# Two x loads trade queues at the start of a fused attention and MLP kernel, and ScalarE's first DMA waits for a GpSimd memset

## The chip, the cores and the metric

The kernel runs on one core of a Trainium2 chip. The metric is the device time of one execution, in microseconds (us).

## What is computed

The inputs are x (2048 tokens of 640 values, bf16), wqkv (640 x 1920), wo (640 x 640), w1 (640 x 1728) and w2 (1728 x 640). The reference, cut to what matters:

```python
xn = layernorm(x)                       # over the 640 values, eps 1e-5, no gain or bias
q, k, v = split_heads(xn @ wqkv)        # 32 heads of 20
phi = lambda t: where(t > 0, t + 1, exp(t)) + 1e-6
kv  = einsum("bhsd,bhse->bhde", phi(k), v)
z   = einsum("bhsd->bhd", phi(k))
o   = (phi(q) @ kv) / (phi(q) . z + 1e-6)
s   = merge_heads(o) @ wo
g   = silu(relu(xn @ w1) @ w2)
out = x + s * g
```

It is linear attention (no softmax over positions) times a gate that an MLP makes, plus the residual.

## The kernel before

The 2048 tokens are 16 tiles of 128 tokens, called t, in four groups j of 512. The 640 values are five blocks of 128, called c or k. Up to eight x tiles are held in `xin` (`x_load`, line 336); xn transposed, so that the values are on the partitions, is `xnT`.

Everything is written in one program order by hand. A small scheduler (`Sched`) keeps, for each engine, the list of its operations in that order, and works out from the tiles that an operation reads and writes which semaphores it has to wait for. It reorders nothing: an engine or a DMA queue executes its own list in order and stops at the first wait that is not met. `extra` adds a wait for a given operation. DMAs are issued from SyncE's queue (SP) or from ScalarE's (ACT); what stands behind a waiting issue on the same engine waits too, ScalarE's own computation included.

The start, which is what the change and the prediction speak of, goes as follows.

- GpSimd sets constants, the first of them `onesM`, 128 x 128 ones (line 344), which TensorE reads only much later, in `z_col`; then the identity that the transposes need, and two more.
- The first loads are issued: x0, x1, x2, the first part of w1 (three of the 128-column blocks f, 480 KB), the second part (two blocks, 320 KB), x3.
- `fill(9)` (line 355): nine matmuls of ones, whose result is not used, while the loads are under way.
- For tiles 0 to 3 the mean of each token is computed alone: `T_mean` (tile 0 on VectorE, line 424; tiles 1 to 3 on ScalarE, line 420). `center` subtracts it (VectorE, line 431), `T_pe` transposes the tile on TensorE (line 437), `T_copy` brings it to `xnT` (lines 444 and 447). The division by the deviation is made up for later.
- `H_first` multiplies the first tiles with the blocks of w1 that have landed (`H_mm`, line 545): tile 0 with blocks 0 to 2, tile 1 with blocks 0 to 2, then, with the second part, blocks 3 and 4.
- The load of the K columns of wqkv is issued when tile 0 has been centred (`held`), and the third part of w1 when tile 2 has been centred. The other loads stand behind these on SyncE's queue.

The order on ScalarE in this stretch is: its two DMA issues, the load of its function table, `T_mean(1)`, two `T_copy`, `T_mean(2)`, `T_mean(3)`, `T_copy`. On VectorE: `T_mean(0)`, `center(0)` in two pieces, `center(1)`, two `T_copy`, `center(2)` and so on. On TensorE: the fill, the transposes of tile 0 and tile 1, `H_first` for tiles 0 and 1.

After that come the K projection with its exponentials, the Q projection and the rest of the MLP's first half, then the sums over the tokens, the MLP's second half, and the output, tile by tile.

Of the kernel before, what the change touches and what calls it, by code (L numbers as in the profile page):

```python
# [211 lines left out]
def bass_recurrent_scan__linear_attn_block__dense_activation_relu__prompt_kernel(  # L212
# [82 lines left out]
    onesM = nc.alloc_sbuf_tensor("onesM", [P, P], bf)  # L295
# [24 lines left out]
    sc = Sched(nc, NDS)  # L320
    nds = [0]

    def dma(E, fn, R=(), W=(), extra=()):
        i = nds[0]
        nds[0] += 1
        return sc.dma(E, fn, i, R=R, W=W, extra=extra)

    def tok(t):
        return slice(P * t, P * (t + 1))
# [4 lines left out]
    def x_load(t, extra=(), E="SP"):  # L334
        sl = t % XR
        return dma(E, lambda eng: eng.dma_start(xin[:, sl, :], x2[tok(t), :]), W=[("xin", sl)], extra=extra)
# [4 lines left out]

    cones = nc.const_aps.tensor(1.0, [P, P], bf)
    cwide = nc.const_aps.tensor(1.0, [P, 512], bf)
    sc.op("POOL", lambda eng: eng.memset(onesM[:, :], 1.0), W=[("onesM",)])
    sc.op("POOL", lambda eng: eng.memset(ident[:], 0.0), W=[("ident",)])
    sc.op("POOL", lambda eng: eng.affine_select(out=ident[:], in_=ident[:], compare_op=ALU.not_equal,
                                                fill=1.0, base=0, pattern=[[-1, P]], channel_multiplier=1),
# [14 lines left out]
    def w1_load(i, extra=(), E="SP"):  # L362
        w_load(w1_sb[:, :, W1C[i]:W1C[i + 1]], B_w1[:, W1C[i]:W1C[i + 1]], ("w1", i), extra, E)

    def w1_part(f):
        return [i for i in range(NP) if W1C[i] <= P * f < W1C[i + 1]][0]

    x_load(0)
    x_load(1, E="ACT")
    x_load(2)  # L370
    w1_load(0, E="ACT")
    w1_load(1)
    x_load(3)
# [335 lines left out]
    for j in range(1, J):  # L709
# [11 lines left out]
        for n, (kind, jj, f) in enumerate(blocks):  # L721
# [19 lines left out]
            else:  # L741
                if n == 0:
                    for t in range(4):
# [4 lines left out]
                        W=[("wo", 0)], extra=[last_norm[0]])  # L748
                    dma("SP", lambda eng: eng.dma_start(wo_sb[0:VR, VC - 1, :], A_wo[D - VR:D, :]),
                        W=[("wo", 1)], extra=[last_norm[0]])  # L750
# [11 lines left out]
    for a in range(2):  # L762
# [3 lines left out]
            W=[("w2", a)], extra=[lastX])  # L766
    for u in range(2):
        dma("SP", lambda eng, u=u: eng.dma_start(w2l[64 * u:64 * (u + 1), :], B_w2[NF * P:FF, :]),
            W=[("w2l", u)], extra=[lastX])
# [235 lines left out]
```

## Time and profile before

| what | before |
|---|---|
| time, median of 3 runs | 221.51 us (221.26 to 221.65) |
| the profiled execution's own time | 221.12 us |
| its span (first to last instruction) | 219.4 us |
| TensorE busy | 215.5 us, 98% |
| VectorE, ScalarE, GpSimd busy | 114.4, 87.5 and 43.5 us |
| DMA moved | 24.51 MB, mean 112 GB/s |

The times in the profile's rows are microseconds from the start of the span. In a row of the timeline the first number is the start, the second the time from there to the end of the last of the merged instructions; `PE` is TensorE's matmuls and `PEld` its weight loads, `SPq` and `ACTq` are the DMA issues on SyncE's and ScalarE's queues. Matmuls overlap, so a busy TensorE is not one at its peak. Brackets give the idle time of the engine before the row, and what ended it.

In a row of DMA issues the last number is the median time from issue to landing. In a row of the table of stretches stand, after the stretch and its length, the busy times of TensorE's matmuls, TensorE's weight loads, VectorE, ScalarE and GpSimd with their instructions in brackets, the clock that TensorE was granted, the busy share of the DMA engines, and GB/s. In the rows of the DMA queues, q1 is SyncE's queue and q10 ScalarE's, with packets, MB and the share of the 16 DMA engines' time.

### The profile page before, as it was taken

The page shows a single profiled execution, that of the slowest core. Times are in us where ns is not written, and L with a number is a line of the kernel's source. Part 1 is how long each engine was busy: PE and PEld are TensorE (multiplying, and loading weights), DVE is VectorE, ACT ScalarE, POOL GpSimd, SP SyncE. Part 2 cuts the span into 40 slices and gives each one's busy share as a digit, 9 for nine tenths or more (in the row PEclk, how much of TensorE's full clock was granted, in tenths as well). Part 3 has the DMA queues.
Part 4 walks back from the last instruction along what each step waited for, and adds up shares of the span by engine and source line. Part 5 has one row for each costly group of instructions (what it writes and reads, how often), then busy time and mean ns, then how long its engine had stood idle before and what let it go on. Part 6 is the DMA issues. An engine that isn't in the chain of part 4 may idle for free.

```text
span 219.4 us, 3577 instructions
## 1 busy us (share of the span) xinstructions
PE 215.5 (98%) x1489; PEld 134.2 (61%) x1489; DVE 114.4 (52%) x196; ACT 87.5 (40%) x143; POOL 43.5 (20%) x66
## 2 busy tenths in 40 slices
PE   8999999999999999999999999999999999999994
PEld 2975654555545554444477778777767776777673
DVE  2778857789676999987700007503322222314053
ACT  4587765576656575555421114531021102110300
POOL 2153101279024998600000000000000000000001
PEclk9999999999999999999999999999999999999999
DMA  6996581350012206800079968377110110000002
GB/s 212 300 382 155 127 225 57 71 45 6 0 30 60 33 1 121 167 3 0 0 228 362 261 202 326 93 241 269 60 63 1 60 33 30 30 31 33 30 30 90
DMA packets 28812, 24.51 MB, mean 112 GB/s; under 512 B 11812, under 2 KB 28156, under 8 KB 28796
## 3 DMA queue, kind: packets, MB, share of 16 engines
q1 hardware_dynamic: 27852, 23.53, 37.6%
q10 hardware_dynamic: 944, 0.75, 1.1%
q8 instruction: 11, 0.18, 0.3%
q14 instruction: 5, 0.04, 0.1%
HBM read 15.75 MB, written 5.24 MB: 96 GB/s over the span
## 4 chain that ended last, share of the span: by engine, by line
PE 96%; DMA 1%; DVE 1%; issue 0%
PE psT L845 26%; PE psT L545 26%; PE psT L891 10%; PE psT L790 10%; PE psT L462 10%; PE psT L530 10%; DMA reg<-in_A_x_dram 1%; PE psT L861 1%; PE psT L567 1%; PE psT L801 1%; PE psT L812 1%; PE psT L437 1%; PE psT L648 1%; DVE ek L424 0%; DVE reg L906 0%; DVE reg L898 0%
## 5 line engine op out<-in xcount | busy, mean ns | idle before, releaser
L545 PE MATMUL psT<-reg 128*128 128x512 bf16 (+1 forms) x335 | 61.7, 331 | 0.0
L845 PE MATMUL psT<-reg,hT 128*128 128x320 bf16 x416 | 60.1, 299 | 0.0
L845 PEld LDWEIGHTS psT<-reg,hT 128*128 128x128 bf16 x416 | 40.4, 98 | 16.4 <-issue 1.1
L545 PEld LDWEIGHTS psT<-reg 128*128 128x128 bf16 x335 | 28.5, 98 | 25.6 <-issue 0.4
L913 DVE TENSOR_TENSOR reg<-psT,reg 128x640 bf16<-128x640 f32 x15 | 12.4, 825 | 54.0 <-PE psT L891 54.0
L552 ACT ACTIVATE hT<-psT 128x512 bf16<-128x512 f32 x52 | 30.7, 599 | 15.8 <-PE psT L545 15.7
L879 ACT ACTIVATE reg<-psT 128x640 bf16<-128x640 f32 (+1 forms) x13 | 8.4, 661 | 44.3 <-PE psT L845 24.9
L898 POOL TENSOR_TENSOR reg<-reg 128x256 bf16<-128x256 bf16 x1 | 0.7, 668 | 124.4 <-DVE reg L906 124.4
L530 PE MATMUL psT<-reg 128*128 128x512 bf16 x100 | 24.9, 379 | 0.0
L462 PE MATMUL psT<-reg 128*128 128x320 bf16 x160 | 24.2, 299 | 0.0
L471 POOL TENSOR_TENSOR zacc<-zacc,reg 128x640 f32<-128x640 f32 x16 | 23.7, 1484 | 1.9 <-DVE reg L505 1.0
L891 PE MATMUL psT<-reg,pqT 128*128 128x320 bf16 (+2 forms) x165 | 24.0, 295 | 0.0
L790 PE MATMUL psT<-reg 128*128 128x320 bf16 x160 | 21.9, 299 | 0.0
L462 PEld LDWEIGHTS psT<-reg 128*128 128x128 bf16 x160 | 15.5, 98 | 8.3 <-DVE ek L489 0.3
L891 PEld LDWEIGHTS psT<-reg,pqT 128*128 128x128 bf16 x165 | 16.0, 98 | 5.8
L790 PEld LDWEIGHTS psT<-reg 128*128 128x128 bf16 x160 | 15.7, 98 | 6.2
L540 DVE SCALAR_TENSOR_TENSOR pqT<-er 128x512 bf16<-128x512 bf16 x20 | 17.1, 854 | 0.7
L530 PEld LDWEIGHTS psT<-reg 128*128 128x128 bf16 x100 | 9.7, 98 | 11.6 <-DVE er L538 0.6
L537 ACT ACTIVATE er<-psT 128x512 bf16<-128x512 f32 x20 | 12.0, 598 | 8.9 <-PE psT L530 8.1
L538 DVE TENSOR_SCALAR er<-psT 128x512 bf16<-128x512 f32 x20 | 13.6, 678 | 3.1 <-ACT er L537 3.1
L395 DVE BATCH_NORM_STATS2 stats<-reg 128x6 f32<-128x320 bf16 x32 | 13.9, 477 | 1.0 <-DMA reg<-in_A_x_dram 1.0
L505 DVE TENSOR_TENSOR reg<-ek 128x640 bf16<-128x640 bf16 x16 | 13.5, 843 | 1.5 <-ACT ek L496 1.0
(63 smaller groups left out, 133.9 us busy)
## 6 DMA issues: line engine op xcount, KB each, us to landing
rscr<-rden SPq DMA_DIRECT2D x4, 640.0 KB, 10.7
reg<-rscr SPq DMA_DIRECT2D x5, 512.0 KB, 6.1
reg<-in_A_x_dram SPq DMA_DIRECT2D x4, 640.0 KB, 6.9
reg<-in_A_x_dram SPq DMA_DIRECT2D x15, 160.0 KB, 3.3
out_dram<-reg SPq DMA_DIRECT2D x15, 160.0 KB, 1.8
reg<-in_A_wqkv_dram SPq DMA_DIRECT2D x2, 800.0 KB, 6.6
reg<-in_B_w_dram SPq DMA_DIRECT2D x1, 1120.0 KB, 5.7
reg<-in_B_w_dram SPq DMA_DIRECT2D x1, 960.0 KB, 8.2
```

What stands on the lines that cost most here:

```text
L395: sc.op("DVE", lambda eng, a=a: eng.bn_stats(stats[:, t, a, :], xv[:, HN * a:HN * (a + 1)]), R=[("xin", t % XR)], W=[("stats", t, a)])
L462: fns.append(lambda eng, a=a, k=k: eng.matmul(ps[b + a][:, 0:HN], lhsT=xnT[:, k, tok(t)], rhs=wqk[:, k, D + HN * a:D + HN * (a + 1)], star ...
L471: sc.op("POOL", lambda eng: eng.tensor_tensor(out=zacc[:, :], in0=zacc[:, :], in1=pk[:, t, :], op=ALU.add), R=[("zacc",), ("pk", t)], W=[( ...
L505: sc.op("DVE", lambda eng: eng.tensor_tensor(out=pk[:, t, :], in0=e_, in1=r_, op=ALU.add), R=[("ek_e", es), ("ek_r", es)], W=[("pk", t)])
L530: sc.group("PE", [(lambda eng, k=k: eng.matmul(ps[b], lhsT=wqk[:, k, P * f:P * (f + 1)], rhs=rhs(k), start=(k == 0), stop=(k == C - 1))) f ...
L538: sc.op("DVE", lambda eng: eng.tensor_scalar(out=r_, in0=ps[b], scalar1=0.0, scalar2=1e-6, op0=ALU.max, op1=ALU.add), R=[("ps", b), ("er_e ...
L540: sc.op("DVE", lambda eng: eng.scalar_tensor_tensor(out=pqT[:, f, schunk(j)], in0=e_, scalar=1.0, in1=r_, op0=ALU.min, op1=ALU.add), R=[(" ...
L545: return sc.group("PE", [(lambda eng, k=k: eng.matmul(ps[b][:, lo:hi], lhsT=w1_sb[:, k, P * f:P * (f + 1)], rhs=xnT[:, k, 512 * j + lo:512 ...
L552: sc.op("ACT", lambda eng: eng.activation(out=hT[:, f, schunk(j)], in_=ps[b], func=ACTF.Relu), R=[("ps", b)], W=[("hT", j, f)])
L790: fns.append(lambda eng, t=t, a=a: eng.matmul(ps[b + a][:, 0:HN], lhsT=xn[:, t, P * k:P * (k + 1)], rhs=pk[:, t, HN * a:HN * (a + 1)], sta ...
L845: sc.group("PE", [(lambda eng, f=f, n=n: eng.matmul(ps[b + n][:, 0:HN], lhsT=hT[:, f, tok(t)], rhs=w2_sb[:, f, HN * n:HN * (n + 1)], start ...
L891: sc.group("PE", [(lambda eng, c=c, pb=pb, lo=lo, hi=hi: eng.matmul(ps[pb][:, 0:hi - lo], lhsT=pqT[:, c, tok(t)], rhs=wf[:, c, lo:hi], sta ...
```

## The change

Before, SyncE issued x0 and x2 and ScalarE issued x1, each as its first work. Now x1 goes out from SyncE right behind x0, in the slot that x2 had, and x2 goes out from ScalarE in the slot that x1 had. Besides, x2's issue waits for GpSimd's memset of `onesM` (`made`), and with it all that stands behind it on ScalarE, the first of which is the first part of w1. The other issues stay on their queues and in their order. What is computed doesn't change. The inserted line moves the numbers of all lines behind it by one.

```diff
-    sc.op("POOL", lambda eng: eng.memset(onesM[:, :], 1.0), W=[("onesM",)])
+    made = sc.op("POOL", lambda eng: eng.memset(onesM[:, :], 1.0), W=[("onesM",)])
...
     x_load(0)
-    x_load(1, E="ACT")
-    x_load(2)
+    x_load(2, [made], "ACT")
+    x_load(1)
     w1_load(0, E="ACT")
     w1_load(1)
     x_load(3)
```

## The prediction

> **What bounds the kernel now.** I read the page first, then a table of four stretches, then the chain of waits in the first 16 us, then the timeline of the first 6 us engine by engine, and last the DMA issues one at a time.
>
> ```profile
> span 219.4 us, 3577 instructions
> ...
> PE 215.5 (98%) x1489; PEld 134.2 (61%) x1489; DVE 114.4 (52%) x196; ACT 87.5 (40%) x143; POOL 43.5 (20%) x66
> ```
>
> ```profile
> 0.00:5.70 5.70, 4.81 (x19) 1.78 (x19) 1.84 (x6) 2.50 (x4) 1.44 (x9) 1.00 0.69 217
> 5.70:80.00 74.30, 74.30 (x486) 42.49 (x483) 58.41 (x118) 48.27 (x83) 31.11 (x49) 1.00 0.43 109
> 80.00:110.00 30.00, 30.00 (x177) 13.70 (x175) 25.60 (x29) 15.96 (x27) 10.30 (x8) 1.00 0.27 53
> 110.00:219.40 109.40, 106.38 (x816) 76.24 (x813) 28.57 (x45) 20.77 (x30) 0.67 (x1) 1.00 0.38 124
> ```
>
> The second number of a stretch is TensorE's busy time. From 5.70 us to 110 us it equals the stretch, so TensorE waits for nobody there, and after 110 us only 3.0 us are missing (the output tail among them). The kernel is a TensorE chain, and whatever moves the first real matmul moves the end by as much. The change touches only the first loads, so the question is when that first matmul starts.
>
> ```profile
> 0.79 2.87 DMA reg<-in_A_x_dram
> ...
> 3.69 0.84 DVE ek L424 x2
> ...
> 4.55 0.30 DVE reg L431
> ...
> 4.89 0.98 PE psT L437 x10
> 5.87 1.72 PE psT L545 x30
> ```
>
> This chain starts with x0's load: it lands at 0.79 + 2.87 = 3.66, VectorE takes its mean and subtracts it, and TensorE begins the transposes at 4.89. The chain names one cause only, so I looked at the neighbours:
>
> ```profile
> 0.79 0.20 POOL L344 MEMSET onesM<- 128x128 bf16 x1 [0.29 <-POOLq L990]
> ...
> 0.80 0.40 ACTq L336 DMA_DIRECT2D reg<-in_A_x_dram  x1
> ...
> 0.83 4.00 PE L355 MATMUL psT<-const-bfloat16-1.0 128*128 128x512 bf16 x9 [0.83 <-PEq L990]
> ...
> 1.23 0.47 ACTq L339 DMA_DIRECT2D reg<-in_B_w_dram  x1
> ...
> 1.71 0.43 SPq L339 DMA_DIRECT2D reg<-in_B_w_dram  x1
> 1.72 1.28 ACT L420 ACT_TABLE_LOAD   x1 [1.72 <-PEq L990]
> ...
> 3.88 0.74 ACT L420 ACTIVATE ek<-reg 128x640 bf16<-128x640 bf16 x1 [0.87 <-DMA reg<-in_A_x_dram]
> ...
> 4.52 0.19 ACT L420 ACTIVATION_READ_ACCUMULATOR ek<-reg 128x1 f32 x1
> ...
> 5.09 0.38 SPq L339 DMA_DIRECT2D reg<-in_A_wqkv_dram  x1
> ...
> 5.75 1.83 PE L545 MATMUL psT<-reg 128*128 128x128 bf16 x30
> ```
>
> ```profile
> 4.19 0.63 PE L355 MATMUL psT<-const-bfloat16-1.0 128*128 128x512 bf16 x1
> ```
>
> ```profile
> 4.98 0.38 DVE L431 TENSOR_SCALAR reg<-reg,mean 128x640 bf16<-128x640 bf16 x1
> ```
>
> ```profile
> 5.41 0.28 PEld L437 LDWEIGHTS psT<-ident,reg 128*128 128x128 bf16 x5
> 5.72 0.24 PEld L545 LDWEIGHTS psT<-reg 128*128 128x128 bf16 x4
> ```
>
> ScalarE computes x1's mean from 3.88 to 4.71 as soon as x1 is there. VectorE could then centre x1 at about 4.74, but it is still busy with x0 and does so at 4.98. So x1 has 0.24 us to spare. Its transposes load at 5.41, 0.05 us after the centring ends at 5.36, and the first H matmul's weights at 5.72, 0.31 us after the first transpose. That H matmul also needs the first part of w1. The landings, one issue each (KB, us from issue to landing):
>
> ```profile
> reg<-in_A_x_dram SPq DMA_DIRECT2D x1, 160.0 KB, 2.9
> ```
>
> ```profile
> reg<-in_A_x_dram ACTq DMA_DIRECT2D x1, 160.0 KB, 3.1
> ```
>
> ```profile
> 1.25 0.42 SPq L336 DMA_DIRECT2D reg<-in_A_x_dram  x1
> ```
>
> ```profile
> reg<-in_A_x_dram SPq DMA_DIRECT2D x1, 160.0 KB, 3.0
> ```
>
> ```profile
> reg<-in_B_w_dram ACTq DMA_DIRECT2D x1, 480.0 KB, 4.4
> ```
>
> ```profile
> reg<-in_B_w_dram SPq DMA_DIRECT2D x1, 320.0 KB, 4.9
> ```
>
> They are, in order: x0 (issued at 0.79, SyncE), x1 (0.80, ScalarE, there at 3.9), x2's issue row and its landing (1.25, SyncE, there at 4.25), the first w1 part (1.23, ScalarE, there at 5.63) and the second (1.71, SyncE, there at 6.6). The first w1 part is there 0.1 us before the first H matmul begins. So three things are due together at 5.72: x0's chain, x1's chain with 0.24 us to spare, and w1's first part with next to none.
>
> **The change part by part.** Nothing is added to any compute engine. Two x loads swap queues, and ScalarE's first issue waits for the memset at line 344.
>
> *The wait on ScalarE.* The memset ends at 0.79 + 0.20 = 0.99. With a hand-over of 0.05 us (as from the centring's end to the transpose's weights) ScalarE issues x2 at about 1.05 instead of issuing x1 at 0.80. Queued behind it are the first w1 part (1.23 becomes 1.48) and the table load (1.72 becomes 1.97, ending at 3.25). The table load stays hidden, since nothing on ScalarE can start before x1 lands; that cover is gone only if x1 were to land before 3.25. On SyncE the second x load still goes out at 1.25 and the second w1 part at 1.71, so nothing behind it there moves.
>
> *x0 lands sooner.* For 0.25 us x0 has the DMA engines to itself, where x1 went out with it before. The bounds are the 2.87 us of now and that of a lone x load later on:
>
> ```profile
> 19.80 0.33 SPq L336 DMA_DIRECT2D reg<-in_A_x_dram  x1
> ```
>
> ```profile
> reg<-in_A_x_dram SPq DMA_DIRECT2D x1, 160.0 KB, 2.4
> ```
>
> So x0 lands between 3.2 and 3.66; since its rival comes 0.25 us later and not at all, I take the middle, 3.43. The transposes would then be ready 0.23 us sooner, at 4.66. The fill matmuls allow 4.62 at the earliest: the last starts at 4.19 and they follow each other every 0.42 us (nine in the row at 0.83, so eight steps from there to 4.19). So at most 0.27 us can be had here, and only if x1 and w1 are as early.
>
> *x1 lands later.* It takes x2's old slot, 0.45 us later than its own was. Bounds: as a lone load 1.25 + 2.4 = 3.65, and as x2 did 1.25 + 3.0 = 4.25. I take 4.2, near the upper one: x0 and x2 are now issued ahead of it, the same two tiles' worth as were ahead of x2. ScalarE's mean then runs from 4.23 to 5.06 (0.83 us from the rows at 3.88 and 4.52), the centring from 5.09 to 5.47, the transposes load at 5.52, the first H matmul at 5.83. The 0.24 us to spare are used up and 0.11 us are lost; at 4.25 it is 0.16 us.
>
> *The first w1 part.* Its issue moves by 0.25 us. If it lands by the bytes ahead of it (three x tiles before as after, engines full), it stays at 5.63; if it keeps its 4.4 us, it lands at 5.88. Which is nearer? Between 3.8 and 4.5 us, this is what the queues moved:
>
> ```profile
> DMA packets 324, 0.25 MB, mean 353 GB/s; under 512 B 2, under 2 KB 324, under 8 KB 324
> ```
>
> I leave that row's split by queue to the rival below; its rate says that the engines were full while this part flowed, which speaks for the bytes. I take 5.75, the middle, and with 0.1 us from landing to weights the first H matmul starts at 5.85.
>
> *Sum.* The latest of 4.66 + 0.83 (x0's chain), 5.83 (x1) and 5.85 (w1) is 5.85, against 5.72: +0.13 us. The gain on x0 is not lost by a fault, it just ends in a wait for x1 and w1. Between the ends: both at their early ends gives 5.72 (w1) and 5.71 (x1 with the slack used), so 0; both at their late ends 5.98, so +0.26. The wqkv load, released by x0's centring at 5.09, may go out 0.2 us sooner; no TensorE stall after 5.70 waits for it, so that is worth nothing. The profiled execution took 221.12 us, 1.72 above its span, and 221.12 + 0.13 = 221.25. The median of the runs is 221.51, 0.39 above the profiled one, and on it the sum is 221.64, which I round to 221.7 since more can go late than early.
>
> **The rivals.** *Slower: the second w1 part gets among the first.* Before, ScalarE had issued the first part (1.23 to 1.70) when SyncE began the second (1.71). Now the first is issued from 1.48 to 1.95 and the second from 1.71 to 2.14, so half of the first part's issue overlaps. If half of the second part (160 KB) goes ahead, the first lands 0.16 MB / 353 GB/s = 0.46 us later, at 6.09, and the H matmul starts at 6.19: +0.47 us. If all of it does, 0.93 us: +0.94 us. The middle gives 221.51 + 0.7 = 222.2. It decides from a landing past 6.06 (5.72 + 0.44 - 0.10). Against it stands the split by queue of the same window, 3.8 to 4.5 us:
>
> ```profile
> q10 hardware_dynamic: 322, 0.25, 106.6%
> q1 hardware_dynamic: 2, 0.00, 0.2%
> ```
>
> q10 is ScalarE's queue, q1 SyncE's. The second part had been issued at 1.71 and yet SyncE's queue moved two packets: the order of issue held, though the two queues were free to alternate. For it speaks that the lead that kept them apart shrinks from 0.48 to 0.23 us, and that how two large loads share when their issues overlap is not seen in this trace. On these grounds I give it about a third of the chance.
>
> The Trainium skill, DMA: Bandwidth & Descriptors, Queues, rings and completion order, says that each DMA engine takes turns between the queues it has work for, a packet at a time. By that rule the two w1 parts would alternate as soon as both are issued, in both kernels, and this rival would be the forecast. The row above does not agree with it for these two loads.
>
> *Faster: the early x0 carries through.* It needs x1 there by 3.83 and w1's first part by 5.36; then the H matmul starts at 4.62 + 0.83 = 5.45, which is -0.27 us, or 221.24. That by itself is no difference that a measurement of this kernel shows (0.2%, 0.44 us). To be more it would take all four starts of the first 6 us closing up (TensorE's missing 0.89 us of the first stretch, 0.83 of them before its first matmul, leave nothing of the kind) or a gain later that the busy rows do not show; 220.9 then. Little speaks for it.
>
> *The change does nothing:* the wait costs as much as x0 gains, x1 lands by 4.09 and w1 at 5.63. 221.5, inside the same bucket as the forecast.
>
> **How the numbers follow.** Forecast (0 to +0.26 us) with the do-nothing case and the small gain: 0.57, all within 0.2%. The w1 rival: 0.35. Faster by over 0.2%: 0.08. The likeliest time is 221.7. Its own range is 221.2 (small gain) to 221.9. With the rival taken to its middle and a little over, the range reaches 222.4; beyond it lies the whole second part going first. Below 221.2 I leave the 0.08.
>
> **What would show it.** In the changed kernel: the first x transposes start at 4.6 to 4.7 instead of 4.89 (x0 sooner); ScalarE's first mean starts at 4.1 to 4.3 instead of 3.88 and VectorE waits for it before x1's centring (x1 later); the second group of transposes loads at 5.45 to 5.55 instead of 5.41; the first H matmul starts at 5.75 to 5.95. From 5.7 to 110 us TensorE stays full. The forecast is wrong if x1 is there by 3.9, if the first w1 part lands after 6.06, if SyncE's queue moves w1's second part before ScalarE's has finished the first, or if a wait shows after 6 us that was not there before.

## The result, and the profile after

| | before | after |
|---|---|---|
| median | 221.76 us (221.09 to 224.09, 22 runs) | 222.97 us (222.09 to 226.43, 22 runs) |
| ratio | | 1.0046, 95% interval 1.0024 to 1.0068 |

The change made the kernel slower, by 1.0 us on the ratio, and the median lies above the forecast range of 221.2 to 222.4. The ratio is taken over executions within 1.5% of each kernel's fastest, and the medians over all of them, of which the changed kernel has more long ones. Timed a second time beside the first variants, the changed kernel had a median of 223.97 us (222.37 to 226.47) and a ratio of 1.0077 (1.0049 to 1.0105). The profile shown here is of that second time, of an execution of 224.35 us; the one of the first time, of 226.43 us, shows the same wait, longer.

This execution is not an ordinary one. Of the 34 timed executions of the changed kernel, 12 had a mean granted clock of 0.985 to 0.992 (223.95 to 226.47 us), like the one shown, whose clock dips. The other 22, at 0.998 to 1.0, had a median of 222.67 us, 0.9 to 1.0 us above the kernel before (221.76 and 221.71 beside them): the loss is there without the dip. Three of these 22 were long as well (224.30, 226.04 and 226.33 us), and no profile shows why.

Of the page, two lines (span, TensorE's granted clock in 40 slices of 5.6 us), then the table of stretches around the place where the clock dips:

```profile
span 222.6 us, 3577 instructions
...
PEclk9699999999999999999999999999999999999999
```

```profile
3.50:7.40 3.90, 1.99 (x15) 0.77 (x13) 2.48 (x8) 2.20 (x6) 0.00 (x0) 1.00 1.02 321
7.40:10.90 3.50, 3.50 (x35) 3.50 (x36) 0.00 (x0) 0.83 (x2) 0.00 (x0) 0.51 1.04 340
10.90:14.00 3.10, 3.10 (x59) 3.10 (x57) 2.78 (x9) 0.70 (x1) 0.80 (x2) 1.00 1.07 376
```

The span is 3.2 us longer. From 3.5 to 7.4 us TensorE works only half of the time. Then, from 7.4 to 10.9, it runs at 0.51 of its clock and gets through 35 matmuls in 3.5 us, where the stretch behind has 59 in 3.1 us. The chain of waits names the cause (start, us, what):

```profile
0.78 0.20 POOL onesM L344
...
1.43 5.81 DMA reg<-in_B_w_dram
7.24 0.14 issue
7.37 3.35 PE psT L546 x30
```

Before, the chain began with x0's load. Now it begins with the memset, goes through ScalarE's queue, and the longest link is the load of w1's first part: 5.81 us, landing at 7.24. In the timeline:

```profile
1.43 0.46 ACTq L339 DMA_DIRECT2D reg<-in_B_w_dram  x1
...
1.71 0.43 SPq L339 DMA_DIRECT2D reg<-in_B_w_dram  x1
...
3.24 0.82 DVE L425 TENSOR_SCALAR_CACHE_REDUCE ek<-reg 128x640 bf16<-128x640 bf16 x1 [3.24 <-DMA reg<-in_A_x_dram]
...
4.44 0.40 PEld L438 LDWEIGHTS psT<-ident,reg 128*128 128x128 bf16 x5 [0.52 <-DVE reg L432]
...
5.39 0.28 PEld L438 LDWEIGHTS psT<-ident,reg 128*128 128x128 bf16 x5 [0.56 <-DVE reg L432]
...
7.37 1.86 PE L546 MATMUL psT<-reg 128*128 128x128 bf16 x16 [1.52 <-DMA reg<-in_B_w_dram]
```

The x part of the change works: x0's mean starts at 3.24 instead of 3.69, the first transposes at 4.44 instead of 4.89, and x1's transposes at 5.39, where they were. Then TensorE waits for w1. The landings are, in order, x0, x2, x1 and the two w1 parts:

```profile
reg<-in_A_x_dram SPq DMA_DIRECT2D x1, 160.0 KB, 2.4
reg<-in_A_x_dram ACTq DMA_DIRECT2D x1, 160.0 KB, 2.6
reg<-in_A_x_dram SPq DMA_DIRECT2D x1, 160.0 KB, 2.8
reg<-in_B_w_dram ACTq DMA_DIRECT2D x1, 480.0 KB, 5.8
reg<-in_B_w_dram SPq DMA_DIRECT2D x1, 320.0 KB, 5.7
```

And the split by queue between 3.8 and 4.5 us, where before ScalarE's queue had 322 packets and SyncE's 2:

```profile
q10 hardware_dynamic: 239, 0.18, 88.4%
q1 hardware_dynamic: 43, 0.02, 10.9%
```

The second part now flows beside the first, and the rate is 294 instead of 353 GB/s.

The account of this execution's 3.2 us: the first H matmul starts at 7.37 instead of 5.75, 1.62 us later. Then 3.4 us at half clock do the work of 1.7. Together 3.3.

### The profile page after: what moved, and what is told of

The parts are those of the page before. It is cut to its first block, busy times and chain, and to the rows that moved or that the text cites. A ratio compares the mean times of both kernels' runs of the same rounds, so it can differ in the third digit from the quotient of the medians.

```text
span 224.7 us, 3566 instructions
## 1 busy us (share of the span) xinstructions
PE 216.9 (97%) x1478; PEld 136.6 (61%) x1489; DVE 114.4 (51%) x196; ACT 87.3 (39%) x143; POOL 43.5 (19%) x66
## 4 chain that ended last, share of the span: by engine, by line
PE 95%; DMA 3%; issue 0%; DVE 0%; POOL 0%; ACTq 0%; POOLq 0%
PE psT L546 26%; PE psT L846 25%; PE psT L892 10%; PE psT L463 10%; PE psT L791 10%; PE psT L531 10%; DMA reg<-in_B_w_dram 3%; PE psT L862 1%; PE psT L568 1%; PE psT L802 1%; PE psT L813 1%; PE psT L649 1%; PE psT L438 0%; DVE reg L907 0%; DVE reg L899 0%
## 5 line engine op out<-in xcount | busy, mean ns | idle before, releaser
L546 PEld LDWEIGHTS psT<-reg 128*128 128x128 bf16 x335 | 30.7, 104 | 28.4 <-issue 3.1
L531 PE MATMUL psT<-reg 128*128 128x512 bf16 x98 | 24.4, 380 | 0.1
L463 PEld LDWEIGHTS psT<-reg 128*128 128x128 bf16 x160 | 15.6, 98 | 8.2
L791 PEld LDWEIGHTS psT<-reg 128*128 128x128 bf16 x160 | 15.7, 98 | 6.2
L531 PEld LDWEIGHTS psT<-reg 128*128 128x128 bf16 x100 | 9.7, 98 | 11.7 <-DVE er L539 0.6
## 6 DMA issues: line engine op xcount, KB each, us to landing
rscr<-rden SPq DMA_DIRECT2D x4, 640.0 KB, 10.9
```

The costliest lines, as they stand in the source:

```text
L463: fns.append(lambda eng, a=a, k=k: eng.matmul(ps[b + a][:, 0:HN], lhsT=xnT[:, k, tok(t)], rhs=wqk[:, k, D + HN * a:D + HN * (a + 1)], star ...
L531: sc.group("PE", [(lambda eng, k=k: eng.matmul(ps[b], lhsT=wqk[:, k, P * f:P * (f + 1)], rhs=rhs(k), start=(k == 0), stop=(k == C - 1))) f ...
L546: return sc.group("PE", [(lambda eng, k=k: eng.matmul(ps[b][:, lo:hi], lhsT=w1_sb[:, k, P * f:P * (f + 1)], rhs=xnT[:, k, 512 * j + lo:512 ...
L791: fns.append(lambda eng, t=t, a=a: eng.matmul(ps[b + a][:, 0:HN], lhsT=xn[:, t, P * k:P * (k + 1)], rhs=pk[:, t, HN * a:HN * (a + 1)], sta ...
```

## The experiments

Each variant was timed on one chip with the others of its group and the kernel before. For each are given the median, the ratio to before with its interval, and from its profile how long the first w1 part took from issue to landing (before: 4.4 us, changed: 5.8) and when the first H matmul began (before: 5.75 us, changed: 7.37).

**The changed kernel again, and its two halves.**

> The changed kernel once more, for a profile of an ordinary execution and its time beside the variants. Theory A (overlapping issue): the first w1 part, issued from 1.43 to 1.89 us, and the second, issued from 1.70 to 2.13, share the making of their descriptors, so both flow at once; the first part then lands near 6.6 us instead of 5.6 and the first H matmul starts near 6.7 instead of 5.72: about +1.0 us, ratio about 1.0045. Theory B (x1 is the late one): x1 lands at 4.2, the first part of w1 by 5.9, the H matmul starts at 5.85 to 5.95, +0.1 to +0.3 us. Theory C (bare delay of ScalarE's queue): the first part lands 0.2 us later than before, because its issue is 0.2 us later, +0.2 us.

The first w1 part landed at 7.24, x1 at 4.07. The first is later than theory A had it, the second is what B had, and x1 delays nothing.

```diff
-    x_load(2, [made], "ACT")
+    x_load(2, E="ACT")
```

> x1 on SyncE behind x0 and x2 on ScalarE, but without the wait. ScalarE then issues at 0.80 and 1.23 as before, and the first w1 part is issued before the second begins. Theory A: no overlap, the first part lands near 5.6 us, the H matmul starts at 5.75 to 5.9 because of x1 alone, time +0.0 to +0.2 us (ratio 1.000 to 1.001). Theory B: x1 still lands at 4.2 to 4.3, so the same time as the full change, about +1.0 us. Theory C: no delay, no loss.

221.49 us median, 0.9987 (0.9963 to 1.0010): no difference. Landing and first H matmul, then the split from 3.8 to 4.5 us:

```profile
reg<-in_B_w_dram ACTq DMA_DIRECT2D x1, 480.0 KB, 4.4
```

```profile
5.94 1.84 PE L546 MATMUL psT<-reg 128*128 128x128 bf16 x30
```

```profile
q10 hardware_dynamic: 331, 0.25, 107.7%
q1 hardware_dynamic: 4, 0.00, 1.1%
```

The split of packets is that of before. H starts 0.19 us later, and the chain of waits of this run shows that it is x1:

```profile
1.25 3.07 DMA reg<-in_A_x_dram
...
4.34 0.84 ACT ek L421 x2
```

So theory B's mechanism exists and costs 0.2 us in the profile, too little to be seen in the time.

```diff
-    x_load(1, E="ACT")
+    x_load(1, [made], "ACT")        # in the kernel before; made as in the change
```

> x1 stays on ScalarE and x2 on SyncE, but ScalarE's first issue waits for the memset. The issue of the first w1 part moves to about 1.43 and overlaps that of the second. Theory A: the first part lands near 6.6 us and the loss is that of the full change, +0.8 to +1.1 us (ratio 1.0035 to 1.005). Theory B: x1 lands at about 4.0, within its 0.24 us to spare, so no loss, 0.0 to +0.1 us. Theory C: +0.2 us.

223.12 us, 1.0042 (1.0019 to 1.0064): the whole loss, with every x load on its old queue. In its profile (an execution of 225.37 us, one of its four longest, with the clock at 0.992) the first part took 6.7 us:

```profile
reg<-in_B_w_dram ACTq DMA_DIRECT2D x1, 480.0 KB, 6.7
```

```profile
8.24 0.94 PE L545 MATMUL psT<-reg 128*128 128x128 bf16 x14 [2.35 <-DMA reg<-in_B_w_dram]
```

The wait is the cause; the order of the x tiles is not. That x0 lands early (it did here too, at 3.10) is not the cause by itself: in two runs below, the second part after x0 and the one queue, it landed as early, and H began by 5.94. C had forecast +0.2 us here; the ratio gives +0.9.

**Keeping the second part away.** First by 0.6 us (SyncE's issue of it waits for the last memset, 2.30 instead of 1.71):

```diff
-    w1_load(1)
+    w1_load(1, [last_set])          # last_set: the memset of zacc
```

> The full change, with SyncE's issue of the second w1 part (and x3 behind it) held until GpSimd's last memset of the setup, about 2.3 us, so that it no longer overlaps the issue of the first part. Theory A: the first part flows alone again and lands at 5.6 to 5.8 us, the second at about 6.9, in time for its use at 7.65; the time is that of before, +0.0 to +0.3 us. Theories B and C: x1 and the first part's issue are as late as in the full change, so nothing comes back: +1.0 us as measured for the full change.

222.77 us, 1.0063 (1.0034 to 1.0092): nothing came back, against theory A as it stood. Yet the profile shows that the two parts no longer flowed side by side at first:

```profile
q10 hardware_dynamic: 313, 0.24, 107.5%
```

```profile
reg<-in_B_w_dram ACTq DMA_DIRECT2D x1, 480.0 KB, 5.4
```

```profile
6.95 1.83 PE L546 MATMUL psT<-reg 128*128 128x128 bf16 x30 [0.75 <-DMA reg<-in_B_w_dram]
```

SyncE's queue moved nothing from 3.8 to 4.5. The trace has 16 arrivals for each of these loads, as many as there are DMA engines. Of the first part's, 15 came by 5.60 us, as before, where all 16 came by 5.62, and the last at 6.81; it alone set the time. In the first profile of the changed kernel the last arrival of the first part came 1.9 us behind the other 15 (8.45 and 6.59), and the last of each of the next three loads 1.8 us behind its others. This fits one DMA engine that had fallen behind; which engine an arrival belongs to is not shown. In the profile above, of 224.35 us, the arrivals are spread (7 by 5.66, the last two at 7.20 and 7.24).

So the second part was then held until the first piece of x0 is centred:

```diff
-    w1_load(1)
-    x_load(3)
...
-    center(0, 0, 2)
+    first_c = center(0, 0, 2)
+    w1_load(1, [first_c])
+    x_load(3)
```

> The full change, with SyncE's issue of the second w1 part and of x3 held until VectorE has centred the first piece of x0, about 4.3 us, when the first part has nearly landed. Theory A (the second part shares the engines with the first): the first part has nothing beside it and all 16 of its arrivals come by 5.7, the first H matmul starts near 5.8, time +0.0 to +0.4 us over before (the second part then lands near 7, about when it is needed). Theory D (the first part's own issue, which overlaps x1's on the other queue, leaves its descriptors late on some engines): one or more of the 16 arrivals still come after 6.5, H near 6.9, +1.0 us or more.

222.25 us, 1.0024 (0.9992 to 1.0056), the fastest execution at 221.43, within 0.3 us of before's fastest. The first part is back:

```profile
reg<-in_B_w_dram ACTq DMA_DIRECT2D x1, 480.0 KB, 4.4
```

```profile
5.94 1.83 PE L544 MATMUL psT<-reg 128*128 128x128 bf16 x30
```

All 16 arrivals came by 5.81. With SyncE's queue moving nothing from 3.8 to 5 us, no arrival stays behind: theory A in a narrower form, and not D, since x1's issue overlaps the first part's here as well. The variant also moves the K columns' load, issued at 5.40; it goes out at 4.64 in the changed kernel (its release is x0's centring) and at 5.09 before. That this load is what comes in is a rival that this run doesn't rule out; the run below with the w1 parts in step speaks against it, since there it is issued at 5.20 and the first part is late all the same. The price comes elsewhere. The profiled execution, of 224.61 us, the longest of its twelve, lost its time after 14 us, when TensorE waited for a K evacuation whose VectorE stood behind a late x tile:

```profile
DVE stats L394 <- DMA reg<-in_A_x_dram: 2.5, 1, 2.5
PEld psT L461 <- DVE ek L488: 2.1, 1, 2.1
```

**One queue.**

```diff
-    x_load(2, [made], "ACT")
     x_load(1)
-    w1_load(0, E="ACT")
+    w1_load(0)
+    x_load(2)
     w1_load(1)
```

> All six first loads on SyncE: x0, x1, first part, x2, second part, x3; ScalarE issues none and waits for nothing. The first part's issue is then later than in any other variant, near 1.7 to 2.15 us, but no two issues overlap. Theory A and theory D both: no sharing, all 16 arrivals close together, the first part by 5.3 to 5.7 (one x tile less ahead of it), H at 5.6 to 5.85, time -0.2 to +0.2 us against before. Theory C (the bare lateness of the issue costs): the first part lands 0.5 us later than before, +0.4 us or more.

222.45 us, 1.0036 (1.0001 to 1.0071). In the profile the start behaves as expected: x0 took 2.2 us from issue to landing, x1 2.4, and the first part, issued only at 1.70, took less than in any other variant:

```profile
reg<-in_B_w_dram SPq DMA_DIRECT2D x1, 480.0 KB, 4.0
```

```profile
5.86 1.83 PE L546 MATMUL psT<-reg 128*128 128x128 bf16 x30
```

In this execution the bare lateness of the issue costs nothing, nor does the early x0: the span is 219.5 us, as before's. But it is the shortest span of the twelve, whose others are 219.8 to 222.9 us, three of them with a mean clock of 0.990 to 0.992 (224.34 to 224.80 us). The ratio is +0.8 us, which is what C expected (+0.4 or more), so the times do not refute C; the profile does so for one execution. (That one took 222.31 us, 2.8 us outside its span against 1.7 before.) What the others lost is left open.

**The first part ahead of x2 on ScalarE.**

```diff
-    x_load(2, [made], "ACT")
+    w1_load(0, [made], "ACT")
     x_load(1)
-    w1_load(0, E="ACT")
+    x_load(2, E="ACT")
```

> The full change with the two issues on ScalarE swapped: the first w1 part at 1.02 us after the wait, x2 behind it at about 1.5. The second part goes out from SyncE at 1.70, 0.2 us after the first part's issue has ended. Theory A: no overlap with the second part, the first part lands by 5.4, H at 5.6 to 5.8, time -0.2 to +0.1 us. Theory D: x1's issue (1.25 to 1.66) still overlaps the first part's, late arrivals after 6.3, +0.6 us or more.

223.62 us, 1.0057 (1.0028 to 1.0085): theory A's forecast fails and D's number comes in (+1.3 us on the ratio), though not by D's arrivals after 6.3, since the first part's last came at 5.94. The landings of x1 and the first part:

```profile
reg<-in_A_x_dram SPq DMA_DIRECT2D x1, 160.0 KB, 4.5
reg<-in_B_w_dram ACTq DMA_DIRECT2D x1, 480.0 KB, 4.9
```

x1's load took 4.5 us instead of 2.8: now the short load is the late one. The chain of waits goes through x1, whose mean starts at 5.78, and H began at 7.60.

**Keeping TensorE busy.** Six unused matmuls behind x1's transposes, the bridge:

```diff
+    sc.group("PE", [(lambda eng: eng.matmul(ps[7], lhsT=cones, rhs=cwide, start=True, stop=True)) for _ in range(6)],
+             W=[("ps", 7)])
     T_copy("ACT", 1, 0, 2, 0)
```

> The full change with six more fill matmuls behind the transposes of x1, so that TensorE does not stand idle while the first w1 part is late; their result is not used. They take 6 x 0.22 = 1.3 us at full clock, from about 5.7 to 7.0. If the slowest executions of the full change (224 to 226 us) come from TensorE's clock dropping to half after the idle, they disappear or shrink and all executions lie between 222.3 and 224; if the slowest come from the late data alone, they stay at 224 to 226. The fast ones become slower, H starting at about 7.0 at the earliest, +1.2 us or more.

222.98 us, all executions between 222.41 and 223.51, where the changed kernel had 222.37 to 226.47. H begins at 7.01 in its profile and the clock does not dip:

```profile
PEclk9999999999999999999999999999999999999999
```

None of the twelve had a mean clock under 0.998, where 12 of the changed kernel's 34 had. In the two profiles of the changed kernel the loss is the late data and the clock that drops after the idle, and with the idle filled nothing above 223.5 was left. The ratio, 1.0044 (1.0019 to 1.0068), stays near the change's first 1.0046. The fill ends at 7.17 and holds H back, for the first part had landed at 6.51: its loads are issued as in the changed kernel, and this landing differs from execution to execution (7.24 and 8.45 in the two profiles of it). A landing at 6.51 would let H begin at about 6.65 (0.14 us later, as in the chain above), 0.9 us later than before, which is near the loss of the executions without the dip.

**Both queues late together.** The same wait also on x0's issue, so that SyncE and ScalarE begin in step, at 1.02:

```diff
-    x_load(0)
+    x_load(0, [made])
```

> The full change, with the same wait also on SyncE's first issue (x0), so that both queues begin together again, only 0.23 us later than without a wait. Theory F (what costs is that ScalarE's issues stand 0.2 us out of step with SyncE's, so that the first w1 part and the second flow side by side): the step between the queues is back as before, the 16 arrivals of the first part come within 0.6 us of each other, everything is 0.2 us later than in the swap alone, time +0.1 to +0.4 us (ratio 1.0005 to 1.002). Theory G (the wait itself, or a later start, is what costs): +1.0 us or more as in the full change.

222.14 us, 1.0023 (1.0003 to 1.0042), a third to a half of the full change's loss, and with +0.5 us a little over what theory F had. First part, split and first H matmul:

```profile
reg<-in_B_w_dram ACTq DMA_DIRECT2D x1, 480.0 KB, 4.3
```

```profile
q10 hardware_dynamic: 268, 0.21, 90.5%
q1 hardware_dynamic: 32, 0.03, 11.2%
```

```profile
6.10 1.84 PE L546 MATMUL psT<-reg 128*128 128x128 bf16 x30
```

(SyncE's 32 packets are the rest of x1, which here goes out 0.2 us later too: between 4.25 and 4.75 us its queue moved none.) The first part takes 4.3 us again, and H is 0.16 us behind the swap alone, for 0.22 us of later start. So half of the cost or more comes from ScalarE's queue being late against SyncE's, as theory F had it; G, with +1.0 us or more, fails.

**The w1 parts in step.** The kernel before, with only the first part held until the identity is drawn:

```diff
-    w1_load(0, E="ACT")
+    w1_load(0, [drawn], "ACT")      # drawn: the affine_select of ident
```

> The kernel before, with x0, x1 and x2 as they were, and only the first w1 part held on ScalarE until GpSimd has drawn the identity, about 1.70 us, the moment at which SyncE issues the second part. Theory A or F (the two parts flow side by side when their issues overlap): full overlap, the first part's arrivals spread over more than a microsecond and the last comes at 6.5 us or later, time +0.8 to +1.5 us, though x0 and x1 land exactly as in the kernel before. A theory in which x0's early landing or x1's late one costs: no loss beyond the 0.5 us by which the issue moved.

226.03 us, 1.0206 (1.0179 to 1.0233), more than expected:

```profile
reg<-in_B_w_dram ACTq DMA_DIRECT2D x1, 480.0 KB, 6.3
```

```profile
q1 hardware_dynamic: 350, 0.18, 94.6%
q10 hardware_dynamic: 6, 0.00, 1.9%
```

```profile
8.17 0.49 PE L545 MATMUL psT<-reg 128*128 128x128 bf16 x6 [2.19 <-DMA reg<-in_B_w_dram]
```

```profile
8.50:12.00 3.50, 3.50 (x37) 3.50 (x35) 0.22 (x1) 0.16 (x2) 0.00 (x0) 0.51 1.01 326
```

From 3.8 to 4.5 us the second part went ahead of the first. Here the lead is zero, and the second part takes first place. H begins 2.4 us later than before and the clock then falls to half, which costs another 1.7 us; together 4.1, for a span 4.0 us longer. The mean clock was 0.985 to 0.992 in all six executions.

**A candidate.** The first part alone on ScalarE, after the second memset, everything else on SyncE:

```diff
     x_load(0)
-    x_load(1, E="ACT")
-    x_load(2)
-    w1_load(0, E="ACT")
+    x_load(1)
+    w1_load(0, [second], "ACT")
+    x_load(2)
```

> A version that keeps x0's early landing: SyncE issues x0, x1, x2, the second part and x3; ScalarE issues the first w1 part alone, when GpSimd has set its second constant (about 1.18 us), so in step with x1's issue at 1.25. If issues in step let the short load through first and the long one follow alone, x0 lands near 3.0, x1 near 3.7 to 4.0, the first part by 5.5, H at 5.4 to 5.7, time -0.3 to 0.0 us against before. If the first part flows beside x1 and x2 as it did with its issue at 1.02, x1 lands after 5 us and H starts after 6.5: +0.8 us or more.

223.34 us, 1.0072 (1.0045 to 1.0098); x1 took 4.1 us and the first part 4.8, H began at 7.17, 1.4 us later than before. TensorE then got through 35 matmuls in the 3.46 us from 6.84 to 10.30, the pace of half clock in the changed kernel's profile (35 in 3.50), though the table gives 1.00 for this stretch and the mean clock of the execution is 0.999. So a mean clock near 1 does not show that the start ran at full clock. No version here beats the kernel before.

## Why the prediction was wrong

**Right.** The bound: TensorE's chain, moved by its first H matmul. The issue times (1.05, 1.48, table load 1.97 forecast; 1.02, 1.43, 1.92 measured). x1's lateness: 4.2 forecast, 4.07 and 4.32 measured, and the 0.1 to 0.2 us that it costs alone (0.19 in the profile of the swap alone). That the gain on x0 ends in a wait. It was larger than I took it: x0 landed 2.4 us after its issue, the end of the bounds that I had put for a lone load, not the middle.

**The step that failed** is the term of the first w1 part. I took 5.75, between 5.63 (by the bytes ahead) and 5.88 (by its own latency); it measured 7.24 in the profile above, 6.51 in the bridge's and 8.11 in that of the wait alone. Neither of my bounds was one, since both assumed that nothing behind it in issue would come in beside it. The mechanism stood among the rivals, with a landing past 6.06 as its mark, and got 0.35 with a middle of +0.7 us. The measured +1.0 us is near its far end of +0.94, where all of the second part goes first, but that the numbers meet is partly luck. The rival counted bytes, and by them the landing could not pass 5.63 + 0.93 = 6.56; it came at 7.24 because some of the arrivals were much later than the others, and with the second part 0.6 us later and nothing from SyncE's queue between 3.8 and 4.5 us, one late arrival was enough for a landing at 6.81.

What I weighed wrongly was the row of packets, 322 against 2. I read it as a rule, that the order of issue holds, when it was the outcome of one timing. With the lead cut from 0.48 to 0.28 us SyncE's queue moved 43 packets in the same stretch, and with no lead 350. The section Queues, rings and completion order of the Trainium skill's page DMA: Bandwidth & Descriptors has a DMA engine take turns between the queues, a packet at a time. None of the three splits from 3.8 to 4.5 us looks like turns: 322 against 2 before, 239 against 43 in the changed kernel, 6 against 350 with the parts in step. The nearest is the changed kernel's from 4.5 to 5 us, 153 against 106.

**The second thing** I had not priced at all: the clock. I looked at TensorE's wait as its only cost, but an idle of 1.5 us and more in this place was followed, in each of the five profiles that have one (both of the changed kernel, the wait alone, the first part ahead of x2, the parts in step), by a stretch at half clock, which cost 1.7 us in the profile above. It is on top of the 1.0 us and does not make it: 22 of the 34 executions show no dip in their mean clock. Nor does every idle of that length bring the fall: 1.63 us of it ahead of 17.85 us, in the run with the second part after x0, did not. The Trainium skill's page TensorE: Matmul & The Clock Gate, What's actually happening, puts the fall after at least one idle window of about 3.4 us. If that means a window without work, this trace does not agree: in the 3.9 us ahead of the fall TensorE was idle only half of the time, 1.99 us being busy, and the longest idle was 1.5 us. That the idle is the cause is shown by the bridge run, in which the clock held in all twelve executions.

**What stays open.** The runs show that ScalarE's lag against SyncE makes the first part late, that it lands on time when the second part is issued only at 4.40, and that most of its 16 arrivals may be on time while one or a few are late. They do not show why arrivals fall behind when the queues are out of step and not when they are in step. Each variant has one profile, and landings differ between executions of one kernel, so a landing here is one sample. A reading that no run tests: a load goes first if its issue ends first. In the kernel before x2's issue ends at 1.66 and the first part's at 1.70, and x2 lands in 3.0 us. In the candidate the first part's ends at 1.62 and x1's at 1.66, and x1 needs 4.1. It does not account for the changed kernel, where the first part's issue ends at 1.89 and the second's at 2.14 and the first is late all the same.

## What to carry to other kernels

A wait put on one of two DMA queues to let a single load go first also shifts everything behind it against the other queue, and that was worth more (1 us) than the load's gain (0.45 us). Before a load is given a bound, list what will be in flight on the other queue beside it, and take as the late bound no less than that all of it goes first; here the landing came later still. Where TensorE's early wait may grow to 1.5 us, as in the five profiles with the fall, add the clock's fall to its price.

## What was unexpected of the hardware

A delay of 0.2 us in an issue lengthened the load by 0.7 to 2.3 us (5.1, 5.8 and 6.7 us from issue to landing against 4.4, in the profiles of the bridge, the changed kernel and the wait alone). In the candidate the first w1 part was issued 0.09 us ahead of x1 on the other queue, and x1's load took 4.1 us, against 2.8 in the changed kernel, where it was issued ahead of that part. Two loads of w1 issued together, 0.8 MB in all, kept the first H matmul until 8.17 us, and flowed at 262 GB/s from 3.8 to 4.5 us, below the 353 GB/s of the kernel before. In the profile with all loads on a single queue they took 2.2 and 2.4 us for x0 and x1, and 4.0 us for the 480 KB, the least for that load in any run here.
